# Key loads of a decode attention kernel moved to ScalarE's DMA queue, with new durations in the plan

## Chip, core and metric

One core of a Trainium2 chip. The metric is the device time of one execution in microseconds (us), lower is better. With one core there is no die to compare. Most executions of the kernel before lie within 0.3% of one another. A difference of over 2%, clear of noise, counts as faster or slower.

## The reference, cut to what matters

Two layers of decode attention with a key and value cache that is the same in both, each followed by a small feed-forward network. There are 8 batches, one query position, 32 query heads on 8 key-value groups, 8192 cached positions, head size 128, and everything is bfloat16.

```python
def _A_ref(x, k_cache, v_cache, wq, wo):          # cut
    q = (x @ wq).reshape(B, 1, 32, 128)...
    scores = einsum("bhqd,bhkd->bhqk", q, k) * (128 ** -0.5)
    o = einsum("bhqk,bhkd->bhqd", softmax(scores), v)
    return o... @ wo

x = x + _A_ref(_layernorm(x), A_k_cache, A_v_cache, A_wq, A_wo)
x = x + _B_ref(_layernorm(x), B_w1, B_w2)         # silu feed-forward
x = x + _A_ref(_layernorm(x), A_k_cache, A_v_cache, A_wq, A_wo)
x = x + _B_ref(_layernorm(x), B_w1, B_w2)
```

One pair of batch and group has 2 MB of keys and 2 MB of values. A query costs little arithmetic, so the work is moving the caches.

## The kernel before

All 8 groups' keys of a batch stay on the chip (`kts`, eight slots of 2 MB), are scored for layer 0 and later for layer 1, and only then make room for the next batch's keys. So the keys are read once. The values do not stay: they are read once per layer, through a ring of six usable cells of 512 KB. A value load takes one cell (512 KB, rows of 4 KB in each partition) or two (1 MB, rows of 8 KB). A key load has rows of 16 KB.

The order of every instruction on every engine is fixed when the kernel is built. A planner steps through a model of the core (engines with durations, DMA as one wire on which loads go one after the other, ring cells that come free) and writes the instructions down in the order of the model's time. On the chip each engine then follows its list and waits on semaphores.

```python
class Plan:
    RATE = {1: 2.57, 2: 2.51, 4: 2.48}     # us per MB by cells, LAND = 2.0, HOP = 0.1
    PE_SLOW = 1.15                         # every TensorE duration times this
    # ... run(): loads strictly in the order in which they were listed
                if li < len(loads):
                    n = loads[li]
                    at = self.place(idle, n.cells) if n.take else None
                    if n.left == 0 and (at is not None or not n.take):
                        # ...
                        wire = max(wire, now + 0.1) + n.dur
                        heapq.heappush(events, (wire + self.LAND, seq, "done", n))

def load_k(b, g):                          # scored[g]: last scores made from slot g
    n = plan.load(f"k{b}.{g}", 4, lambda: dma(
        sp, slot(g), A_k_cache[b, g]..., ksem[g], writes=[res("kt", g)]),
        scored.get(g, []), ring=False)
    return n

def turns(b, g):                           # VectorE transposes a landed key slot in place
    kn = load_k(b, g)
    for q in range(4):
        # op(dve, lambda: dve.transpose(v, v), ...) planned after kn

# keys(): four score steps on TensorE (8 matmuls each), then a softmax chain:
#   VectorE max -> GpSimd max over partitions -> VectorE own_max -> ScalarE exp -> TensorE swap -> ...
    sn.append(plan.add(f"s{u}.{q}", "PE", 0.3, score, pr - 1, [tn[3], bn] + sn[-1:]))
# values(): four steps on TensorE per group, each reads one ring cell
    n = plan.add(f"v{u}.{P}", "PE", 0.35, pv, pr, [h["exp"], vn, ...] + vs[-1:])
```

SyncE issues every load. It is an in-order engine too: while a key load waits for the last scores of its slot, the value loads listed behind it wait as well (13.2 us at the first turn of a batch, shown below).

## Time and profile before

| | before |
|---|---|
| time, median | 1187.4 us (1186.84 to 1187.71, 3 runs); 1187.56 with a fourth run beside the change |
| profiled span | 1180.7 us |
| bytes moved | 467.13 MB, mean 396 GB/s |
| TensorE, VectorE, ScalarE busy | 60%, 51%, 12% |
| SyncE waiting for a ring cell (for value matmuls to end) | 654.1 us |
| SyncE waiting for scores, before a key load | 155.1 us in 29 waits |

From the page: the DMA engines' mean busy share in 40 slices of the span, what they moved, the queue that did it, and the chain of waits that ended last.

```profile
DMA  9999799999999999999999999999999999999993
GB/s 365 421 419 346 311 420 421 414 403 403 422 411 412 398 381 417 422 408 391 421 421 407 400 412 412 415 411 400 413 415 406 371 393 421 422 410 403 384 354 149
...
q1 hardware_dynamic: 86272, 465.10, 97.8%
...
DMA 76%; PE 16%; issue 4%; DVE 2%; SPq 1%; POOLq 0%; ACT 0%; POOL 0%; DVEq 0%; ACTq 0%
```

Every slice but the first turn of a batch and the end is full of DMA, and the chain runs over DMA for three quarters of the span. One hardware queue (q1) carries all loads. The DMA engines bound this kernel.

SyncE's own waits (who it waited for: us in total, times, longest):

```profile
SPq L91 <- PE ot L842: 654.1, 300, 21.5
SPq L91 <- PE sc L746: 155.1, 29, 13.2
```

The first is the ring: a value load waits until TensorE has used up a cell. The second is what the change goes for. Where it hurts is best seen at the first turn of a batch, in stretches of 4 us (stretch, length, busy time and count of PE, PEld, DVE, ACT, POOL, then TensorE clock, DMA share, GB/s), with SyncE's issues below them:

```profile
120.00:124.00 4.00, 2.27 (x72) 2.11 (x73) 0.74 (x3) 0.20 (x1) 0.56 (x1) 0.50 0.80 313
124.00:128.00 4.00, 3.75 (x100) 2.88 (x104) 0.56 (x3) 0.00 (x0) 0.00 (x0) 0.50 0.04 14
128.00:132.00 4.00, 2.99 (x56) 1.31 (x52) 1.97 (x10) 0.57 (x2) 0.83 (x2) 0.93 0.56 188
```

```profile
104.93 10.49 SPq L340 DMA_DIRECT2D ring<-in_A_v_cache_dram  x4
128.67 0.33 SPq L340 DMA_DIRECT2D kts<-in_A_k_cache_dram  x1
129.05 3.68 SPq L340 DMA_DIRECT2D ring<-in_A_v_cache_dram  x4
```

From 115 to 128.67 us SyncE stands at a key load (one wait for scores of 13.2 us), and the DMA engines fall idle, although value loads go out the moment the key load does: cells had been free.

Landing (from the page's DMA issues: count, KB each, median us from issue to landing):

```profile
ring<-in_A_v_cache_dram SPq DMA_DIRECT2D x260, 512.0 KB, 8.2
kts<-in_A_k_cache_dram SPq DMA_DIRECT2D x64, 2048.0 KB, 11.2
ring<-in_A_v_cache_dram SPq DMA_DIRECT2D x126, 1024.0 KB, 11.0
```

### The profile page before, as it was taken

The numbers are of one execution on the slowest core, as the hardware profiler recorded it, in microseconds if no ns is written. First come the engines' busy times: TensorE is split into PE (matmuls) and PEld (weight loads), VectorE is DVE, ScalarE is ACT, GpSimd is POOL, SyncE is SP. The second block draws the span as 40 slices with busy tenths as digits, with TensorE's granted clock in tenths as the row PEclk, the third lists the DMA queues.
The fourth block names the chain that finished last, engine by engine and source line by source line (L and its number), as shares of the span: only waits on it lengthen the run. The fifth ranks groups of instructions, "written<-read, shape, count | busy, mean of one in ns | idle before, by whom it ended". The sixth has DMA issues, their size and how long they took to land.

```text
span 1180.7 us, 31675 instructions
## 1 busy us (share of the span) xinstructions
PE 706.9 (60%) x13588; PEld 370.5 (31%) x13588; DVE 597.7 (51%) x1713; ACT 136.9 (12%) x475; POOL 117.3 (10%) x295
## 2 busy tenths in 40 slices
PE   2544555675565755666665755667556575566844
PEld 1322332242332423323332323324233242333423
DVE  5652367625564255733667254752557336663321
ACT  0010011101111110110111111111101111111110
POOL 1000011101110010100111010110001001110110
PEclk9765677657676676756777568765667567675775
DMA  9999799999999999999999999999999999999993
GB/s 365 421 419 346 311 420 421 414 403 403 422 411 412 398 381 417 422 408 391 421 421 407 400 412 412 415 411 400 413 415 406 371 393 421 422 410 403 384 354 149
DMA packets 86413, 467.13 MB, mean 396 GB/s; under 512 B 8944, under 2 KB 14848, under 8 KB 61952
## 3 DMA queue, kind: packets, MB, share of 16 engines
q1 hardware_dynamic: 86272, 465.10, 97.8%
q8 instruction: 107, 1.75, 0.6%
q14 instruction: 34, 0.28, 0.1%
HBM read 465.05 MB, written 0.01 MB: 394 GB/s over the span
## 4 chain that ended last, share of the span: by engine, by line
DMA 76%; PE 16%; issue 4%; DVE 2%; SPq 1%; POOLq 0%; ACT 0%; POOL 0%; DVEq 0%; ACTq 0%
DMA ring<-in_A_v_cache_dram 70%; PE ot L842 7%; PE sc L746 6%; DMA kts<-in_A_k_cache_dram 3%; DMA ring<-in_A_wq_dram 2%; DMA w<-in_B_w_dram 1%; DVE kts L694 1%; PE misc L642 1%; SPq L340 1%; PE ex L864 0%; PE sc L721 0%; PE yt L915 0%; PE misc L510 0%; DVE small L758 0%; PE ex L886 0%
## 5 line engine op out<-in xcount | busy, mean ns | idle before, releaser
L842 PE MATMUL ot<-ring,p 128*8 128x256 bf16 x4096 | 256.6, 365 | 220.8 <-DMA ring<-in_A_v_cache_dram 218.9
L694 DVE STREAM_TRANSPOSE kts<-kts 128x1024 uint32<-128x1024 uint32 x256 | 306.1, 1222 | 35.4 <-DMA kts<-in_A_k_cache_dram 35.3
L746 PE MATMUL sc<-kts,bd 128*32 128x256 bf16 x4096 | 288.6, 406 | 33.8 <-DVE kts L694 21.7
L842 PEld LDWEIGHTS ot<-ring,p 128*8 128x8 bf16 x4096 | 80.0, 92 | 313.9 <-DMA ring<-in_A_v_cache_dram 288.7
L746 PEld LDWEIGHTS sc<-kts,bd 128*32 128x32 bf16 x4096 | 116.3, 117 | 107.4 <-DVE kts L694 32.1
L856 DVE TENSOR_TENSOR part<-ot,p 128x256 bf16<-128x256 f32 x128 | 54.2, 423 | 177.1 <-ACT p L852 98.5
L763 POOL PARTITION_ALL_REDUCE small<-small x128 | 47.8, 373 | 637.4 <-DVE small L759 383.1
L772 ACT ACTIVATE expd<-sc,small 128x256 bf16<-128x256 f32 x128 | 60.7, 474 | 422.1 <-DVE small L767 365.6
L852 ACT ACTIVATE p<-ot 128x256 bf16<-128x256 f32 x128 | 49.1, 383 | 487.7 <-PE ot L842 486.7
L778 PE MATMUL sc<-expd,ident 128*32 128x256 bf16 x512 | 42.3, 318 | 91.1 <-ACT expd L772 88.4
L758 DVE TENSOR_REDUCE small<-sc 128x1 f32<-128x256 f32 x128 | 53.2, 415 | 51.3 <-PE sc L746 51.2
L792 POOL PARTITION_ALL_REDUCE small<-small x128 | 55.3, 432 | 214.2 <-DVE small L788 214.2
L729 DVE TENSOR_TENSOR bd<-sc,mask 128x64 bf16<-128x64 f32 x128 | 27.7, 217 | 83.1 <-PE sc L746 73.9
L785 DVE STREAM_TRANSPOSE p<-sc 128x256 bf16<-128x256 bf16 x128 | 56.9, 445 | 7.3 <-PE sc L778 4.5
L778 PEld LDWEIGHTS sc<-expd,ident 128*32 128x32 bf16 x512 | 15.4, 109 | 121.9 <-ACT expd L772 119.5
L788 DVE TENSOR_SCALAR small<-hm,small 128x4 f32<-128x4 f32 x128 | 26.4, 206 | 33.4 <-ACT expd L772 33.4
L864 PE MATMUL ex<-diag,p 128*128 128x4 bf16 x256 | 26.3, 172 | 23.5 <-DVE part L856 21.2
L915 PE MATMUL yt<-z,ring 128*128 128x4 bf16 x1024 | 36.1, 166 | 6.1 <-DVE z L893 4.5
L915 PEld LDWEIGHTS yt<-z,ring 128*128 128x128 bf16 x1024 | 31.2, 100 | 27.0 <-issue 26.8
L864 PEld LDWEIGHTS ex<-diag,p 128*128 128x128 bf16 x256 | 16.4, 104 | 72.2 <-issue 38.5
L767 DVE SCALAR_TENSOR_TENSOR small<-small,hm 128x4 f32<-128x4 f32 x128 | 19.4, 152 | 37.4 <-POOL small L763 37.2
L759 DVE TENSOR_SCALAR small<-hneg,small 128x4 f32<-128x4 f32 x128 | 29.4, 230 | 4.5
(82 smaller groups left out, 433.9 us busy)
## 6 DMA issues: line engine op xcount, KB each, us to landing
ring<-in_A_v_cache_dram SPq DMA_DIRECT2D x260, 512.0 KB, 8.2
kts<-in_A_k_cache_dram SPq DMA_DIRECT2D x64, 2048.0 KB, 11.2
ring<-in_A_v_cache_dram SPq DMA_DIRECT2D x126, 1024.0 KB, 11.0
ring<-in_A_wo_dram SPq DMA_DIRECT2D x64, 512.0 KB, 11.3
ring<-in_A_wq_dram SPq DMA_DIRECT2D x36, 512.0 KB, 9.7
kts<-in_A_wo_dram SPq DMA_DIRECT2D x2, 2048.0 KB, 15.8
w<-in_B_w_dram SPq DMA_DIRECT2D x2, 1792.0 KB, 13.2
wq<-in_A_wq_dram SPq DMA_DIRECT2D x4, 512.0 KB, 11.2
```

What stands on the lines that cost most here:

```text
L694: op(dve, lambda: dve.transpose(v, v), reads=[], writes=[res("kt", g)], add=(q > 0))
L746: steps.append(lambda t=t, y=y, w=w: pe.matmul(sc[32 * t:32 * t + 32, 0:256], w, kv[:, 2 * t + y, q], start=(q == 0 and y == 0), stop=(q = ...
L758: op(dve, lambda: dve.tensor_reduce(mxr[si], sv, AX.X, ALU.max), reads=[res(*scr)], writes=[res("mxr", si)])
L763: op(pool, lambda: pool.partition_all_reduce(mxa[si], mxp[si], 128, bass.bass_isa.ReduceOp.max), reads=[res("mxp", si)], writes=[res("mxa" ...
L772: op(act, lambda: act.activation(pe_out[:, :], sv, ACT.Exp, bias=bias[si], scale=SM_SCALE, accum_out=rsum[si]), reads=[res(*scr), res("bia ...
L778: steps = [lambda P=P: pe.matmul(sc[32 * P:32 * P + 32, 256:512], src[:, P], pe_out[:, :], start=True, stop=True) for P in range(4)]
L785: op(dve, lambda: dve.transpose(pt[:, :], src), reads=[res(*scr)], writes=[res("p", sm)])
L792: op(pool, lambda: pool.partition_all_reduce(ssa[si], ssm[si], 128, bass.bass_isa.ReduceOp.add), reads=[res("mxp", si)], writes=[res("mxa" ...
L842: steps.append(lambda t=t, c=c, k=k: pe.matmul(ot[32 * t:32 * t + 2 * R, 0:2 * DH], pt[:, k:k + 2 * R], vt[:, c, t], start=(P == 0 and c = ...
L852: op(act, lambda: act.activation(pt[:, :], ot[:, 0:2 * DH], ACT.Copy), reads=[res("ot", o)], writes=[res("p", sm)])
L856: op(dve, lambda: dve.tensor_tensor(part[:, :], ot[:, 0:2 * DH], pt[:, :], ALU.subtract), reads=[res("ot", o), res("p", sm)], writes=[res( ...
L915: steps.append(lambda j=j, dt=dt: pe.matmul(YT[:, dt * R:(dt + 1) * R], w[:, j, dt * 128:(dt + 1) * 128], zt[:, R * j:R * j + R], start=(g ...
```

## The change

The intent is that a key load of batches 1 to 7 should go out as soon as the last scores of its slot are made, and should hold up no value load. So ScalarE, which makes few instructions, issues these 56 loads in its own hardware queue, and the planner lists the two queues apart. The planner also gets TensorE durations nearer to measured ones.

```diff
-    PE_SLOW = 1.15
+    PE_SLOW = 1.0
...
-        self.loads = []
+        self.queues = {"SP": [], "ACT": []}
...
-                if li < len(loads):
-                    n = loads[li]
+                for loads in todo.values():
+                    if not loads:
+                        continue
+                    n = loads[-1]
...
     def load_k(b, g):
-        n = plan.load(f"k{b}.{g}", 4, lambda: dma(
-            sp, slot(g), A_k_cache[b, g].rearrange("(p y) d -> p (y d)", p=128), ksem[g], writes=[res("kt", g)]),
-            scored.get(g, []), ring=False)
-        return n
+        def issue(eng):
+            dma(eng, slot(g), A_k_cache[b, g].rearrange("(p y) d -> p (y d)", p=128), ksem[g], writes=[res("kt", g)])
+
+        if g not in scored:
+            return plan.load(f"k{b}.{g}", 4, lambda: issue(sp), ring=False)
+        n = plan.add(f"kq{b}.{g}", "ACT", 0.4, lambda: issue(act), count[0] - 8, scored[g])
+        return plan.load(f"k{b}.{g}", 4, lambda: None, [n], ring=False, queue="ACT")
...
-            sn.append(plan.add(f"s{u}.{q}", "PE", 0.3, score, pr - 1,
+            sn.append(plan.add(f"s{u}.{q}", "PE", 0.45, score, pr - 1,
...
-            n = plan.add(f"v{u}.{P}", "PE", 0.35, pv, pr, [h["exp"], vn, old or clear_n] + vs[-1:])
+            n = plan.add(f"v{u}.{P}", "PE", 0.4, pv, pr, [h["exp"], vn, old or clear_n] + vs[-1:])
```

More of the change, by code (lines that the diff above doesn't have):

```diff
@@ L152, in add, with load @@
         return n
-    def load(self, name, cells, emit, deps=(), ring=True):
+    def load(self, name, cells, emit, deps=(), ring=True, queue="SP"):
         n = Node(name, "DMA", cells * 0.5 * self.RATE.get(cells, 2.57), emit, 0, deps)
@@ L159, in load @@
         self.nodes.append(n)
-        self.loads.append(n)
+        self.queues[queue].append(n)
         return n
@@ L185, in run @@
         pending = {id(n): i for i, n in enumerate(self.nodes)}
-        loads = list(self.loads)
-        li = 0
+        todo = {q: list(reversed(loads)) for q, loads in self.queues.items()}
         wire = 0.0
@@ L210, in run @@
                         seq += 1
-                        li += 1
+                        loads.pop()
                         moved = True
@@ L238, in run @@
                         heapq.heappush(heaps[o.eng], (o.prio, pending[id(o)], o))
-        assert done == len(self.nodes), (done, len(self.nodes), loads[li].name if li < len(loads) else "")
+        assert done == len(self.nodes), (done, len(self.nodes))
         self.span = now
```

## The prediction

> **What bounds the kernel now.** The DMA engines. The page shows 467.13 MB moved in 1180.7 us, mean 396 GB/s. The table by stretch (20 us each) shows the 16 engines at a share of about 1.0 from 140 to 1100 us, at 400 to 425 GB/s. With only 512 KB value loads (380 to 396 us) they run at 404 to 411, with key loads mixed in (480 to 500 us) at 425. TensorE is busy 60%, ScalarE 12%. The chain of waits is 76% DMA, mostly value loads.
>
> In 4 us stretches, measured against 415 GB/s, the lost time is 3.6 us at the start, 12.5 us between 80 and 140 us (the first turn), 13.4 us in all of 140 to 1100 us, and 24.5 us after 1100 us. The change moves no key load of the first or last.
>
> **What the change moves.** 56 of the 64 key loads (2 MB each) leave SyncE's in-order queue. There they hold up value loads whose ring cells are free: SyncE's own waits show 155.1 us in 29 waits for scores (PE sc). Most of that cost no bandwidth; where it did is visible: at 124 to 128 us the DMA share is 0.04, then a key load goes at 128.67 with value loads right behind it; at 428 to 436 us 297 and 281 GB/s, key load at 432.26; at the turns of a batch (264 to 276, 544 to 556, 820 to 832 us) 320 to 365 GB/s around the first two key loads.
>
> **What it adds.** 56 issues on ScalarE at 0.33 to 0.45 us (SyncE's durations), about 22 us on an engine busy 137. Its waits for scores come just before the exponential of the same scores, so little is blocked. [...]
>
> The plan's PE durations become 0.45 (scores) and 0.40 (values) instead of 0.345 and 0.4025. Busy time per step is 288.6/512 = 0.56 and 256.6/512 = 0.50 us: the scores move nearer the truth. A few us either way.
>
> **Sum (an estimate).** First turn: about 2 ring cells at 1.28 us each (512 KB at 409 GB/s), 2 to 4 us. Later turns and mid-batch holes: about half of the 13.4 us, 5 to 8. New collisions and reordering: minus 2 to plus 3. Net about -9 us of 1187: **1178 us, 1165 to 1190**. Faster by over 2%: 0.08; within 2%: 0.87; slower by over 2%: 0.05.
>
> **What would show each step.** A second hardware queue with 117 MB; SyncE's waits for scores fall under 20 us; no share of 0.04 at 124 to 128 us; mean GB/s 398 to 401; the 415 GB/s loss in 140 to 1100 us falls to 5 to 9; start and tail as before; value loads land later, keys about as now.
>
> **What would make it wrong.** If mixed queues lower the engines' rate; if ScalarE, stuck on a score wait, holds exponentials that TensorE needs at a turn; if early keys leave only six ring cells to fill the turn; or if the better plan closes holes in the tail too.

Minus 2 to 4, minus 5 to 8, and minus 2 to plus 3 come to about -9 us, from 1187 to 1178 us. "About half" of the 13.4 us and the whole last term were estimates of mine that no trace had shown.

## The result, and the profile after

After: 1233.6 us median (1228.53 to 1241.08, 4 runs) against 1187.56 us before (4 runs). The ratio is 1.0393, interval 1.0338 to 1.0447: **slower by 3.9%**. Ratios here are the mean time of one kernel's fast runs over that of the other's of the same rounds, so not quite the ratio of the medians that are quoted.

The same lines of the page, after:

```profile
DMA  9999999999999999999999999999999999999994
GB/s 370 421 409 352 367 378 396 388 387 387 384 409 365 398 386 398 355 389 410 380 406 360 364 395 384 374 391 382 395 366 391 377 395 385 362 390 381 393 377 181
...
q1 hardware_dynamic: 78208, 347.65, 72.8%
q10 hardware_dynamic: 8064, 117.44, 23.6%
...
DMA 59%; PE 24%; DVE 9%; issue 6%; ACT 1%; SPq 1%; POOL 0%; POOLq 0%; ACTq 0%; DVEq 0%
```

The bytes are the same and the new queue (q10) has its 117 MB, but slice after slice mostly moves 360 to 400 GB/s where before mostly moved 400 to 420. DMA's part of the chain fell from 76% to 59%; TensorE and VectorE took it over. The 9s of the DMA row hide this, so GB/s is the row to read.

SyncE's waits, the first turn and the landings, after:

```profile
SPq L91 <- PE ot L846: 843.3, 307, 20.9
```

```profile
120.00:124.00 4.00, 2.21 (x70) 2.04 (x70) 0.66 (x3) 0.20 (x1) 0.55 (x1) 0.50 1.02 406
124.00:128.00 4.00, 3.60 (x96) 2.81 (x100) 0.64 (x4) 0.00 (x0) 0.00 (x0) 0.50 0.81 324
128.00:132.00 4.00, 2.99 (x54) 1.29 (x47) 1.74 (x9) 0.56 (x2) 0.83 (x2) 0.68 0.55 163
```

```profile
ring<-in_A_v_cache_dram SPq DMA_DIRECT2D x260, 512.0 KB, 8.6
ring<-in_A_v_cache_dram SPq DMA_DIRECT2D x126, 1024.0 KB, 8.8
kts<-in_A_k_cache_dram ACTq DMA_DIRECT2D x56, 2048.0 KB, 12.0
```

The intended part worked: SyncE's wait for scores is gone, and the hole at 124 us is filled (324 GB/s instead of 14), though the next stretch is no better (163 GB/s instead of 188). But SyncE now waits 189 us more for ring cells. The medians of landing show nothing of it. Those of the keys rose from 11.2 to 12.0, those of the 1 MB value loads even fell.

Adding up, over stretches of 4 us, what each lacks to 415 GB/s (lost time = 4 us x (415 - GB/s) / 415) gives this table. The last column is the experiment e3, explained below, which has the plan of after in one queue.

| lost time, us | before | after | e3 |
|---|---|---|---|
| 0 to 20 us | 3.6 | 3.5 | 3.9 |
| 80 to 140 us, first turn | 12.5 | 8.5 | 7.8 |
| 140 us to 80 us before the end | 14.2 | 72.7 | 18.7 |
| the last 80 us | 24.5 | 18.3 | 20.7 |
| stretches under 350 GB/s in the third row | 9 of 240 | 50 of 252 | 14 of 239 |

(The span is rounded down to whole stretches for this, so the row of the last 80 us starts at 1100, 1148 and 1096 us.) All of the loss lies in the steady part.

The records of single packets (a packet is one piece of a load: of the 144 packets of a moved key load, 128 are its rows of 16 KB and 16 have 4 bytes) say what form the loss takes. Their times, added up and divided by 16 engines, are 1164.9 us of the span of 1176.8 us in e3, and 1194.0 of 1231.1 us in after. So of the 54 us between the spans, by this count, 25 are idle engines and 29 are packets that took longer. The median packet of each size took the same in both (611 to 612, 309 and 159 ns for 16, 8 and 4 KB). What grew is a tail of slow packets, and why is not shown.

### The profile page after: what moved, and what is told of

It reads as the page before. It is cut to its first block, busy times and chain, and to the rows that moved or that the text cites. A ratio compares the mean times of both kernels' runs of the same rounds, so it can differ in the third digit from the quotient of the medians.

```text
span 1231.1 us, 31624 instructions
## 1 busy us (share of the span) xinstructions
PE 696.1 (57%) x13588; PEld 378.6 (31%) x13588; DVE 590.3 (48%) x1713; ACT 135.1 (11%) x475; POOL 116.8 (9%) x295
## 4 chain that ended last, share of the span: by engine, by line
DMA 59%; PE 24%; DVE 9%; issue 6%; ACT 1%; SPq 1%; POOL 0%; POOLq 0%; ACTq 0%; DVEq 0%
DMA ring<-in_A_v_cache_dram 43%; PE sc L750 12%; DMA kts<-in_A_k_cache_dram 10%; PE ot L846 7%; DVE kts L698 4%; DMA ring<-in_A_wq_dram 3%; DMA w<-in_B_w_dram 1%; PE misc L646 1%; ACT expd L776 1%; DVE p L789 1%; PE sc L725 1%; DVE bd L733 1%; DVE part L860 1%; PE yt L919 1%; DVE small L762 1%
## 5 line engine op out<-in xcount | busy, mean ns | idle before, releaser
L846 PE MATMUL ot<-ring,p 128*8 128x256 bf16 x4096 | 259.6, 362 | 264.6 <-DMA ring<-in_A_v_cache_dram 257.4
L698 DVE STREAM_TRANSPOSE kts<-kts 128x1024 uint32<-128x1024 uint32 x256 | 307.2, 1225 | 41.0 <-DMA kts<-in_A_k_cache_dram 40.9
L846 PEld LDWEIGHTS ot<-ring,p 128*8 128x8 bf16 x4096 | 83.3, 92 | 342.6 <-DMA ring<-in_A_v_cache_dram 313.0
L750 PEld LDWEIGHTS sc<-kts,bd 128*32 128x32 bf16 x4096 | 122.3, 118 | 114.6 <-DVE bd L733 31.5
L878 DVE TENSOR_TENSOR qab<-ex,rc 128x4 bf16<-128x4 f32 x64 | 10.0, 157 | 63.6 <-PE ex L868 63.2
L771 DVE SCALAR_TENSOR_TENSOR small<-small,hm 128x4 f32<-128x4 f32 x128 | 19.2, 150 | 27.8 <-POOL small L767 27.7
```

What stands on the lines that cost most here:

```text
L698: op(dve, lambda: dve.transpose(v, v), reads=[], writes=[res("kt", g)], add=(q > 0))
L750: steps.append(lambda t=t, y=y, w=w: pe.matmul(sc[32 * t:32 * t + 32, 0:256], w, kv[:, 2 * t + y, q], start=(q == 0 and y == 0), stop=(q = ...
L846: steps.append(lambda t=t, c=c, k=k: pe.matmul(ot[32 * t:32 * t + 2 * R, 0:2 * DH], pt[:, k:k + 2 * R], vt[:, c, t], start=(P == 0 and c = ...
```

## The experiments

### e1 to e4: the plan or the queue?

Two things changed at once: the order of all engines' work (the plan) and the hardware queue of the key loads. Four kernels take them apart.

e1 is before with the three durations alone. e2 is after with the old durations. e3 and e4 cross plan and queue:

```diff
 e3, against after: same plan, SyncE issues at the planned place
-        n = plan.add(f"kq{b}.{g}", "ACT", 0.4, lambda: issue(act), count[0] - 8, scored[g])
+        n = plan.add(f"kq{b}.{g}", "ACT", 0.4, lambda: issue(sp), count[0] - 8, scored[g])
 e4, against before: same plan, ScalarE issues at the planned place
-        n = plan.load(f"k{b}.{g}", 4, lambda: dma(
-            sp, slot(g), ...
+        n = plan.load(f"k{b}.{g}", 4, lambda eng=act if g in scored else sp: dma(
+            eng, slot(g), ...
```

Comparing the built programs shows that e3 has the instruction order of after, and e4 that of before, on TensorE, VectorE and GpSimd, row for row.

> The kernel before with the new PE durations in its plan alone (scale 1.0 instead of 1.15, scores 0.45, values 0.40); key loads stay in SyncE's queue. Theory P (the order that the new plan makes is at fault, the queue is innocent) in its form P1, durations: about 1225 to 1235 us. Theory P2 (the order is at fault because key loads are planned apart from the value loads, not because of the durations) and theory Q (two hardware queues share the engines so that value loads starve beside a key load): within 1% of before, 1180 to 1197 us.

> The key loads planned apart and issued by ScalarE, with the plan's old durations. P1: about 1187 us, as before. P2 and Q: 1220 to 1240 us, as after.

> The plan of after to the letter, so the same order on TensorE, VectorE and GpSimd, but the key loads issued by SyncE at their place in the plan: one hardware queue again. P (P1 or P2): 1220 to 1240 us, as after, for the order is the same. Q: within 1.5% of before, 1180 to 1205 us, for value loads issued earlier no longer share with a key load; landing of key loads as the order of issue has it.

> The plan of before to the letter, the same order on every compute engine, but 56 key loads issued by ScalarE in its own hardware queue. P: within 1% of before, 1175 to 1197 us. Q: 1215 us or more, as value loads then starve beside key loads.

| | key loads by SyncE | key loads by ScalarE |
|---|---|---|
| plan of before | before: 1186.85 us (7 runs) | e4: 1235.21 us, ratio 1.0409 (1.0371 to 1.0446) |
| plan of after | e3: 1181.24 us, ratio 0.996 (0.9937 to 0.9983) | after: 1233.6 us, ratio 1.0393 |

e1: 1184.74 us, ratio 0.9998 (0.9944 to 1.0052). e2: 1236.52 us, ratio 1.0437 (1.0393 to 1.0482).

The plan is cleared, in both its parts. The queue alone costs 4%, whichever plan it gets. With the plan of after in one queue the kernel is 0.4% faster than before, which counts as the same by the limit of 2%. This is what the new plan is worth, separate lists and durations together.

The traces of e3 say more. SyncE's waits in it, and its stretch at the first turn:

```profile
SPq L91 <- PE ot L846: 658.1, 304, 21.5
SPq L91 <- PE sc L750: 131.0, 45, 11.7
124.00:128.00 4.00, 3.74 (x100) 2.81 (x101) 0.56 (x3) 0.00 (x0) 0.00 (x0) 0.50 0.81 320
```

The wait for ring cells is back at its value of before, so its 189 us more came with the second queue. SyncE still waits 131.0 us for scores, and yet the DMA engines lose only 18.7 us in the whole steady part: most of the waiting that the change was to remove cost nothing. And the hole at 124 us is filled without a second queue (320 GB/s), by the plan alone.

### e8: is it ScalarE, held by waits?

A key load on ScalarE waits for its scores in ScalarE's own list, in front of exponentials. e8 puts that wait alone into e3:

```diff
-        n = plan.add(f"kq{b}.{g}", "ACT", 0.4, lambda: issue(sp), count[0] - 8, scored[g])
+        n = plan.add(f"kq{b}.{g}", "ACT", 0.4, lambda: (syn.acquire(act, writes=[res("kt", g)]), issue(sp)), count[0] - 8, scored[g])
```

> e3 (the plan of after, key loads issued by SyncE) in which ScalarE also waits for the scores at the place where it issues the key load in after, and issues nothing. Q2: 1215 us or more. Q1: within 0.7% of e3, 1173 to 1190 us.

1180.14 us, ratio 0.994 (0.9911 to 0.997). The waits cost nothing. The other direction, ScalarE's activations holding up the issue, was read from the trace of after: from the end of a slot's last score to the issue of its key load, the median over 56 loads is 0.05 us and the mean 0.34, with only group 7 held (2.4 us on average). In e3 it is 0.09 us. So the issue is not late enough to explain 50 us. Group 7 doesn't explain it either: in e2, and in e9 below, no group is held (0.04 and 0.05 us on average), and both are as slow as after.

### e5 to e7: how the two queues share

When both queues have work, how is it divided? The DMA queues of after from 568 to 576 us (packets, MB, share of 16 engines' time) and from 486 to 492 us:

```profile
q10 hardware_dynamic: 185, 2.77, 81.1%
q1 hardware_dynamic: 181, 0.68, 21.4%
...
q10 hardware_dynamic: 120, 1.70, 66.4%
q1 hardware_dynamic: 116, 0.88, 34.6%
```

The packet counts are about equal in these stretches (185 and 181, 120 and 116), so neither queue moved more packets than the other while both had work. A key packet is a 16 KB row (but for those 16 of 144). In the first stretch the other queue's packets are mostly 4 KB rows, in the second mostly 8 KB ones, and the bytes go about 4 to 1 (2.77 and 0.68 MB) and 2 to 1 (1.70 and 0.88 MB). So here the load with longer rows got the more bytes. The two together still move 432 and 430 GB/s in these stretches. They are good ones: from 506 to 512 us, where the value queue had gaps, all queues together moved 373 GB/s.

```profile
q10 hardware_dynamic: 110, 1.69, 72.8%
q1 hardware_dynamic: 65, 0.53, 21.6%
```

So all packets were counted, from 140 us to 80 us before the end. In after, packets of both queues were under way for 365 us of this, at 402 GB/s on average, against 407 GB/s in e3 over the same part. For 579 us there were only packets of the value queue, at 374 GB/s. Of the 72 us lost against 415 GB/s, 12 fall into the first and 57 into the second. So sharing takes little bandwidth while it lasts (402 GB/s against 407), and most of the loss comes when the key queue is empty.

My theory was then that the values starve beside a key load. If so, smaller key rows should help. e5 cuts each key load into two of every other 4 KB piece, e7 does the same with 2 KB pieces, and e6 is the control of e5 in one queue.

```diff
+            for j in range(2 if late else 1):                 # late: batches 1 to 7
+                cut = (lambda v: v.rearrange("p (a b n) -> p b a n", a=2, b=2)[:, j]) if late else (lambda v: v)
+                dma(eng, cut(slot(g)), cut(A_k_cache[b, g]...), ksem[g], ...)      # a=4 in e7; eng is SyncE in e6
```

> After, with each moved key load cut into two of 1 MB whose rows are 4 KB pieces (every other piece), the size of the pieces of a 512 KB value load. Theory Q1 (the engines take one piece in turn from each queue, so beside 16 KB key pieces a 4 KB value piece gets a fifth of the engines; in the trace of after, 568 to 576 us, 21.4% against 81.1%): value loads get half or more, and the excess over e6, its control in one queue, falls from about 52 us (after minus e3) to 10 to 30 us. Theory Q2 (ScalarE is held by the waits and issues of key loads): the excess stays at 45 to 60 us, and if anything grows, for there are twice the issues.

> Control for e5: the plan of after, key loads by SyncE in one queue (e3) with the same 4 KB pieces. All theories: 4 KB pieces run some 3% slower than 16 KB ones (409 against 423 GB/s), on 117 MB about 10 us: 1185 to 1197 us.

> As e5 with pieces of 2 KB: a value load gets two thirds (512 KB) or four fifths (1 MB) beside a key load. Q1: the loss from sharing falls further, to under 15 us; [...] 1190 to 1225 us. Q2: 1235 us or more.

The shares in these expectations are estimates of mine from the equal packet counts above. For the 3% of e6's, the trace of before has 612 ns for the median packet of 16 KB and 159 ns for that of 4 KB, which is 4% more per byte.

e5: 1337.06 us, ratio 1.1261 (1.1228 to 1.1294). e6: 1198.36 us, ratio 1.0108 (1.0071 to 1.0146), just above its range. e7: 1415.65 us, ratio 1.1923 (1.186 to 1.1987).

The theory missed by a long way. In e5 the keys had 1.76 of 3.20 MB from 614 to 622 us and 1.38 of 3.34 MB from 626 to 634 us, a smaller share than in the stretches of after (2.77 of 3.45 and 1.70 of 2.58 MB), and the loss is larger. (The shares in e7 were not read, and it has no control in one queue, so part of its loss can be the 2 KB pieces themselves.) The excess over the same loads in one queue grows from 52 us (1233.6 - 1181.24) to 139 us (1337.06 - 1198.36). VectorE's waits for key loads (us in total, times, longest) and TensorE's for values show which kind is late, e3 first, then after, then e5:

```profile
PE ot L846 <- DMA ring<-in_A_v_cache_dram: 246.2, 213, 5.2
DVE kts L698 <- DMA kts<-in_A_k_cache_dram: 72.9, 49, 3.2
```

```profile
PE ot L846 <- DMA ring<-in_A_v_cache_dram: 257.4, 128, 7.4
DVE kts L698 <- DMA kts<-in_A_k_cache_dram: 40.9, 21, 3.4
```

```profile
PE ot L851 <- DMA ring<-in_A_v_cache_dram: 153.8, 122, 3.8
DVE kts L703 <- DMA kts<-in_A_k_cache_dram: 246.1, 54, 10.6
```

In e5 the keys are late: from issue to landing they take 16.7 us on average, against 13.0 in e6. They have no spare slot: from a slot's last score over load, transposes and first new score, the time is a loop that every batch goes through. In after it is mostly the values that come in fewer, longer waits. Of all 386 value loads, the slowest tenth took over 13.1 us to land in e3 and over 14.1 us in after, at the same median (8.6 in both). Keys do not land later: they take 11.9 us from issue to landing in after and 12.5 in e3, on average. But the first transpose starts 1.9 us after the landing in after, and at once (0.04 us) in e3. So the transposes come late because VectorE does, with other steps and waits in front of them in its list.

How a wait for a key holds up the rest can be followed in one place of after (timeline, lines left out):

```profile
502.92 0.33 ACTq L341 DMA_DIRECT2D kts<-in_A_k_cache_dram  x1
...
504.81 3.89 SPq L341 DMA_DIRECT2D ring<-in_A_v_cache_dram  x4
...
511.75 2.04 PE L750 MATMUL sc<-kts,bd 128*32 128x256 bf16 x32 [0.33 <-DVE bd L733]
...
514.74 1.25 DVE L698 STREAM_TRANSPOSE kts<-kts 128x1024 uint32<-128x1024 uint32 x1 [2.45 <-DMA kts<-in_A_k_cache_dram]
515.91 0.12 DVE L771 SCALAR_TENSOR_TENSOR small<-small,hm 128x4 f32<-128x4 f32 x1
...
516.13 0.47 ACT L776 ACTIVATE expd<-sc,small 128x256 bf16<-128x256 f32 x1 [8.65 <-DVE small L771]
...
518.10 2.24 SPq L341 DMA_DIRECT2D ring<-in_A_v_cache_dram  x4
```

A key load goes out at 502.92 us, and four value loads from 504.81 us on share with it. Its transposes stand in VectorE's list in front of a softmax step (L771). VectorE waits at them until the load lands at 514.7, so L771, the exponential behind it and the value steps behind that are all late, and SyncE gets its next cells only at 518.10. The load took 11.8 us, no more than the mean key load of e3, so this place shows what a wait for a key does, and not that sharing made this key late. The GB/s of after in these stretches, and of e3 in the same stretches of its own time, where the work isn't exactly the same:

```profile
504.00:508.00 4.00, 2.77 (x52) 1.25 (x52) 3.92 (x11) 1.12 (x4) 0.94 (x3) 0.75 0.89 306
508.00:512.00 4.00, 3.09 (x60) 1.86 (x64) 1.91 (x5) 0.00 (x0) 0.12 (x1) 0.50 0.95 379
512.00:516.00 4.00, 1.79 (x32) 0.83 (x24) 1.52 (x6) 0.00 (x0) 0.37 (x1) 0.89 0.97 359
```

```profile
504.00:508.00 4.00, 0.70 (x12) 0.22 (x12) 2.69 (x6) 0.95 (x3) 0.43 (x1) 0.93 1.00 398
508.00:512.00 4.00, 3.02 (x56) 1.45 (x60) 3.35 (x7) 0.17 (x1) 0.00 (x0) 0.50 1.03 410
512.00:516.00 4.00, 2.52 (x46) 1.13 (x39) 1.15 (x5) 0.67 (x3) 0.37 (x1) 0.65 1.04 410
```

How often the DMA engines ran short of work can be counted as well. From 140 us to 80 us before the end, at most two loads were outstanding (issued and not yet landed) for 8 us in before and 15 us in e3, but for 85 us in e4 and 98 us in after. In these times e4 moved 321 GB/s and after 365.

### e9: does a plan that knows the sharing help?

The planner's model has one wire in the order of issue, which fits one queue (the loads of e3 landed in that order, as counted below). Perhaps the lists are merely wrong for two. e9 lets the heads of both queues run at once in the ratio of their rows.

```diff
-                        wire = max(wire, now + 0.1) + n.dur
-                        heapq.heappush(events, (wire + self.LAND, seq, "done", n))
+                        share(now)          # both heads advance, 16 : 8 : 4 by row length
+                        wire[n.queue].append([n, n.dur + (0 if wire[n.queue] else 0.1)])
+                        ahead(now, seq)     # next end of a head
```

> After with one edit in the plan: instead of one wire in the order of issue, the two queues share it in the ratio of their pieces (16 for a key load, 8 for a 1 MB value load, 4 otherwise), as the trace of after shows it. Theory S (every engine's fixed order was laid out for landings in the order of issue; landings in another order block engines at steps whose data is late, and with a plan that knows the sharing the loss goes): 1180 to 1205 us. Theory B (the sharing itself makes both kinds of load late; six ring cells and one slot per key cannot cover it in any order): 1215 us or more.

1230.52 us, ratio 1.0383 (1.0349 to 1.0417), as slow as after. So a model that ignores the sharing is not the cause, as far as this edit repairs it. In its trace a key takes 12.2 us from issue to first transpose, no more than in e3, but the slowest tenth of value loads takes over 16.7 us.

### e10 and e11: more ring

If both kinds are late now and then, more cells should cover it. To make room for them, these two kernels leave out the second FFN weight, and the second product reads the first weight. Their result is wrong (relative error 0.107 in both).

```diff
-N_CELL = 7
+N_CELL = 10
-    w2_sb = sb([128, FT, D], BF16, "w2")
+    w2_sb = w1_sb[:, :, :].rearrange("p k f -> p (k f)").rearrange("p (t d) -> p t d", t=FT)
```

> After with ten ring cells instead of seven (nine in use instead of six). The room comes from the second FFN weight, which isn't loaded (the result is wrong on purpose, 1.8 MB or about 4 us fewer to move); e11 is its control in one queue. Theory B: with half as much ring again the excess over e11 falls from about 52 us to under 25 us. Theory S without B: the excess stays at 35 to 60 us, for a late key load still blocks engines in their order.

> Control for e10: the plan of after, key loads by SyncE in one queue, ten ring cells, no second FFN weight (result wrong on purpose). All theories: 1165 to 1180 us, for the DMA engines are already at a share of 1.0 in e3 and 4 us of bytes are gone.

e10: 1207.36 us, ratio 1.0187 (1.0153 to 1.022, unclear at the limit of 2%). e11: 1184.45 us, ratio 0.9987 (0.996 to 1.0014). The excess of two queues over one falls from 52 to 23 us, as the buffer theory said. That e11 is not faster than e3 is a miss: nine cells gave one queue nothing, and why is not known.

### e12: interleaving without a second queue

Is it the sharing, or does a second hardware queue cost something of its own? e12 has one queue. It cuts each key load into four contiguous column pieces of 512 KB, which the planner issues in turn with the value loads.

```diff
+        for j in range(4):
+            # issue: dma(sp, slot(g)[:, c], src[:, c], ksem[g], ...) with c the j-th quarter
+            n = plan.load(f"k{b}.{g}.{j}", 1, issue, scored[g], ring=False, queue="ACT")
...
+                    if not loads or (q == "ACT" and turn == "V" and wire > now + 0.5):
+                        continue            # a quarter of a key only after another load, or on an idle wire
```

> One queue (SyncE), but each moved key load cut into four of 512 KB (4 KB pieces), planned and issued in turn with the value loads: about the split that the two queues of e5 make, in a plan that knows it. Theory B (loads that share the engines all land late, whoever shares them): 1225 us or more, clearly over e6 (1198, the same pieces in order). Theory H (sharing is harmless, a second hardware queue costs something of its own): within 1.5% of e6, 1180 to 1215 us.

1288.43 us (median of three runs; the fourth, slow, took 1297.5), ratio 1.0873 (1.0801 to 1.0944), against 1198.36 us (1.0108) for e6, which moves rows of the same size in order. Interleaving in a single queue, in a plan that knows it, costs 90 us, and keys land late as in e5 (15.0 us from the first issue to the last landing, 13.0 in e6, on average). It is not a clean test of sharing, though. Here a quarter can stand behind a value load that waits for a cell, and value loads behind a quarter that waits for scores. SyncE's waits for scores, e12 first, then e6:

```profile
SPq L91 <- PE sc L755: 187.4, 37, 15.7
SPq L91 <- PE sc L755: 127.5, 45, 11.8
```

How much of the 90 us is such blocking is not known. So e12 shows that interleaved issue can lose this much without a second queue, and not that the second queue costs nothing of its own. The 402 GB/s while both queues have packets (above) speak against a large cost of that kind.

### e13 and e14: a larger share for keys

With every value load of 512 KB, keys should get four fifths beside all of them: an estimate from the 2.77 of 3.45 MB that they had beside mostly 4 KB rows in after, where it was 1.70 of 2.58 MB, two thirds, beside mostly 8 KB rows.

```diff
-                a_values(made[v], cells=1 if b >= 0 and i >= len(vs) - 3 else 2)
+                a_values(made[v], cells=1)
-                values(made[v], cells=1 if i < 2 else 2)
+                values(made[v], cells=1)
```

> After with every value load of 512 KB (4 KB pieces), so that a key load gets four fifths beside all of them instead of two thirds beside those of 1 MB. If the key loads are what is late in after, the excess over its control e14 falls below 40 us (after minus e3 is 52); if the value loads are, it grows over 60 us.

> Control for e13 in one queue: e3 with every value load of 512 KB. All theories: 4 KB pieces at 409 instead of 425 GB/s on another 126 MB or so, about 10 us over e3: 1183 to 1200 us.

e13: 1248.68 us, ratio 1.0548 (1.0511 to 1.0586). e14: 1216.65 us, ratio 1.0269 (1.0215 to 1.0324), above what was expected of it, and not explained. The excess is 32 us, under the 40 that was set for "keys are late". It fits the direction of e5, where a smaller share for keys came with a larger loss. But smaller loads also come through the ring in finer steps, and the waits of after (above) point at values. Landings speak against late keys too: they take 11.5 us in e13 and 12.8 in e14, on average. How much of after's 52 us belongs to late keys and how much to late values stays open.

## Why the prediction was wrong

The prediction was 1178 us, 1165 to 1190, with a chance of 0.05 for slower by over 2%. Measured were 1233.6 us, slower by 3.9%, at a mean of 379 GB/s instead of 398 to 401. Its steps, one by one:

- **What bounds the kernel, and the first turn: right.** The hole at 124 us is gone, and the first turn lost 8.5 us instead of 12.5, a gain of 4.0 (predicted 2 to 4). But e3, in one queue, loses no more there (7.8 us), so the plan alone is enough for this gain, without the second queue.
- **SyncE's waits for scores fall under 20 us: right.** They are gone.
- **"Later turns and mid-batch holes: about half of the 13.4 us, 5 to 8": wrong.** The 13.4 us are 14.2 by the sum of the table. Even in one queue (e3) the lost time of the steady part did not fall (18.7 us). The gain of e3 is at the first turn and in the tail.
- **"Start and tail as before": wrong for the tail,** which lost 18.3 us after against 24.5. That the better plan could do this stands among the ways to fail.
- **ScalarE: right.** e8 shows that its waits cost nothing.
- **Plan durations, "a few us either way": right.** e1 has 0.9998.
- **"Value loads land later, keys about as now": the medians were the wrong place to look.** Beside a key load, value loads had a fifth or a third of the bytes (0.68 of 3.45 and 0.88 of 2.58 MB), by row length. The median grew by 0.4 us for 512 KB and fell by 2.2 us for 1 MB. It is the slow tenth that lands later (over 14.1 us, 13.1 in e3).
- **The step that failed: "New collisions and reordering: minus 2 to plus 3".** The collision term is about +50 us: e4 against before, with the same order on TensorE, VectorE and GpSimd, is 48 us (1235.21 - 1186.85), and after against e3 is 52 us. I assumed that nothing is lost when two queues share the engines, and no run had shown that. Little is lost while both have work, that is so: 402 GB/s on average, against 407 in e3. The term left out what the sharing does afterwards, through the ring.
- **What the runs show in its place.** That the second queue costs 4%, whatever the plan, is shown (e3 and e4). So is its form: SyncE waits 189 us more for ring cells, at most two loads are outstanding for 98 us instead of 15 in e3, and more cells halve the excess (e10 against e11). How sharing leads there is my account, and in part argued. In one queue the loads landed in the order of issue (from 140 us to 80 us before the end of e3, no later key or value load landed before an earlier one). With two, keys and values in flight together divided the bytes (2.77 to 0.68 and 1.70 to 0.88 MB), so that one could delay the other. A late landing stops an in-order engine (VectorE for 2.45 us at 512 us of after, with the softmax step behind it), which frees no ring cells (SyncE had its next at 518.10 us), and the six cells did not keep the DMA engines busy meanwhile (98 us with at most two loads outstanding, at 365 GB/s). But the landings of after moved little: keys did not land later, and few values did. Only 11 of 342 value loads were overtaken by over 0.3 us. e5 and e12 lose much by keys that land late, which after does not have. e9 shows that planning for the sharing in this way doesn't avoid the loss.

The prediction named "if mixed queues lower the engines' rate" as a way to fail. That was near, but most of the rate is lost after the collision and not in it (57 of 72 us while the key queue has no packets).

## What to carry to other kernels

In this kernel the one DMA queue, hardly ever short of work (at most two loads outstanding for 8 us in before), was also a schedule: the loads landed in the order in which the lists need them (in e3, none out of order in the steady part). Before giving a class of loads a queue of its own because it blocks others, ask whether the engines are idle while it blocks. Here they were busy (14.2 us lost in the steady part of before), and the second queue, with a ring of six cells and in-order engines, cost more than the blocking did: moving 25% of the bytes (117 of 465 MB) to ScalarE's queue cost 4.1% with the same order on TensorE, VectorE and GpSimd (e4), and with 4 KB key rows 11.5% of the time before (1.1261 - 1.0108). The same rows interleaved instead of in order, in one queue, cost 90 us (e12 against e6), an unknown part of it by blocking in SyncE. Planning the loads apart but issuing them through one queue (e3) kept the small gain of 0.4%. And 131 us of waits in an engine that only issues loads (SyncE in e3) cost little there: the length of a wait is not its cost.
